# A two-layer attention and MLP kernel: the last queries of the first layer in two chunks, the last result block in three pieces, and a new order

## The chip, the cores and the metric

The kernel runs on one core of one Trainium2 chip. Its engines work side by side and meet only at semaphores: TensorE (PE in the profile; its weight loads are PEld), VectorE (DVE), ScalarE (ACT), GpSimd (POOL), and SyncE (SP), which issues the DMAs. The metric is device microseconds of one execution, as the median of several runs; lower is better.

## The reference

The input x has 2048 rows (positions) of 512 numbers. Two layers follow one another, with the same weights, and each has two halves:

```python
x = x + A(layernorm(x))     # attention: 32 heads of 16, causal, window of 256 positions
x = x + B(layernorm(x))     # an MLP over positions
x = x + A(layernorm(x))
x = x + B(layernorm(x))

# A: q, k, v = x @ wqkv;  p = softmax(mask(q k^T / 4));  out = (p v) @ wo
# B: h = layernorm(x);  u = gelu(h^T @ w1 + b1);  y = u @ w2 + b2;  out = y^T
#    w1 is 2048 x 1792, w2 is 1792 x 2048
```

The MLP mixes positions: its first product sums over all 2048 rows, so it can't be finished before the attention of the last row is done.

## The kernel before

Rows are kept as 16 blocks of 128 (x_sb, in bf16). A layer's attention is worked in chunks of queries, counted in units of 64: `CHUNKS` lists (start, length) pairs. The first layer has chunks of 256, 256, 512, 512 and 512 queries, the second layer four of 512.

For each chunk, `attention` (from about L645) takes the tiles of `attention_plan`. A tile holds eight pieces of 64 keys by 64 queries for four heads, side by side, and each goes through five steps: scores on TensorE (L689, 32-row matmuls, four heads at a time), the exponential on ScalarE (L704, two of 128x1024 a tile), masks on GpSimd or VectorE (L725), the product with V on TensorE (L746, 64-row matmuls of 17 columns of weights), and a finish of transpose, reciprocal, product and transpose on VectorE and GpSimd (L766, L770, L772, L777). A chunk of 512 goes through one head group at a time, with five tiles each; a chunk of 256 goes through pairs of head groups, and the two groups of a pair share their third tile, so a pair has five tiles. `wo_block` then multiplies by wo (through the helper at L512), adds to x_sb (L788), and normalises two blocks for the MLP (statistics L470 and L472, reciprocal root L483 on GpSimd, L490 on VectorE).

The first MLP product is split over blocks of rows so that part of it can run under the attention. In the first layer `u_part` sums blocks 0 to 3 and later blocks 4 to 11 as filler matmuls (L512, xh_sb by w1b), and `u_last` adds blocks 12 to 15 (L867), where two column tiles at a time hold two PSUM banks until all four blocks are in. The Gelu follows on ScalarE (L882). The second MLP product (`y_block`, L512 again, and L908) runs in the second layer under the attention's projections and at the end of the kernel alone. The last block of the result goes through `y_last` (L894, output DMA L897).

At the start, `f_warm` (L393) issues 42 matmuls on a constant tile. Meanwhile x and the weights are loaded, the first blocks are normalised and transposed on TensorE (L548), and the first projections follow. GpSimd builds constants and clears two key buffers (L460).

All operations are recorded first, in a graph with their reads, writes and buffers. Then `ORDER`, a compressed list of the operation to take next and of the engine that is to do it, is replayed: it fixes each engine's queue and which buffer each tile gets. The waits follow from the graph. The order was found offline; the kernel holds only its result.

Of the kernel before, what the change touches and what calls it, by code (L numbers as in the profile page):

```python
# [42 lines left out]

def begin_order(n):
# [260 lines left out]
def bass_interleave_layers__sliding_block__mixer_token_mlp__prompt_kernel(  # L305
# [11 lines left out]
    S, D = A_x.shape[1], A_x.shape[2]  # L317
    F = B_w1.shape[1]
# [3 lines left out]
    NFT = F // P  # L322
# [5 lines left out]
    SPLIT = [True, False]  # L328
    STAGED = [(1, 0), (2, 0), (3, 0)]

    CHUNKS = [[(0, 4), (4, 4), (8, 8), (16, 8), (24, 8)], [(0, 8), (8, 8), (16, 8), (24, 8)]]
    PARTS = [[(2, 0, 4), (4, 4, 12)], [(2, 0, 8)]]

    es = ExitStack()
    with es:
        sb = lambda name, shape, d=dt.bfloat16: es.enter_context(nc.sbuf_tensor(name, shape, d))
        x_sb = sb("x_sb", [P, NT, D])
# [14 lines left out]
        uT = sb("uT", [P, NFT, 512])  # L352
# [11 lines left out]
        b2col = sb("b2col", [P, NT], dt.float32)  # L364
# [5 lines left out]
        g = Graph(nc, es)  # L370
        op = g.op
# [17 lines left out]
        warm = Tile(banks)  # L389

        def f_warm(e):
            for _ in range(42):
                last = e.matmul(PS[:, warm.slot, 0:P], lhsT=uT[:, 0, 0:P], rhs=uT[:, 0, 0:P], start=True, stop=True)  # L393
            return last
        op("vector:wm", lambda e: e.memset(uT[:, 0, 0:P], 1.0), writes=["uT0"], cost=100)
# [13 lines left out]
        def load_w(i, a, b):  # L409
# [12 lines left out]
           cost=2600, prio=-1e6)  # L422
# [10 lines left out]
        for h in range(2):  # L433
# [5 lines left out]
               reads=["ident"], writes=[("half", h)])  # L439
# [19 lines left out]
        for k in (1, 2):  # L459
            op("gpsimd:zero", lambda e, k=k: e.memset(kbd[:, k].rearrange("p a b c d -> p (a b c d)").bitcast(dt.float32), 0.0),  # L460
               writes=["kz0"], cost=1900)
# [44 lines left out]
        def fprio():  # L506
            return 1e6 + len(g.ops)
# [10 lines left out]
        def mm_group(kind, dst, n, mk, reads, cols=512, step=2, prio=None, holds=(), after=()):  # L518

            prio = fprio() if prio is None else prio  # L520
            for k0 in range(0, n, step):
                k1 = min(n, k0 + step)

                def f(e, cols32, k0=k0, k1=k1):
                    last = None
                    for k in range(k0, k1):
                        last = matmul(e, cols32, *mk(k), start=(k == 0), stop=(k == n - 1))
                    return last
                rd = reads(k0, k1) if callable(reads) else reads
                op("tensor:" + kind, f, reads=rd, writes=[dst], cost=mm_cost(k1 - k0, cols), prio=prio, holds=holds, after=after, cfg="f",  # L530
                   cls="f", flex=True)
# [354 lines left out]
        def y_last(t):  # L886

            keys, w = w2t[t // 2]
            k = t % 2
            for c in (0, 256):  # L890
                ft = filler(True)
                mm_group("fy", ft, NFT, lambda fc, c=c, ft=ft: (bank(ft)[:, 0:256], w(fc)[:, k * P:(k + 1) * P], uT[:, fc, c:c + 256]),
                         lambda a, b: keys[a // 2:(b + 1) // 2] + [f"uT{fc}" for fc in range(a, b)], cols=256)
                op("vector:resy", lambda e, c=c, ft=ft: e.scalar_tensor_tensor(  # L894
                    x_sb[:, t, c:c + 256], bank(ft)[:, 0:256], b2col[:, t:t + 1], x_sb[:, t, c:c + 256], op0=ALU.add, op1=ALU.add),
                   reads=[ft, "b2", f"x{t}"], writes=[("y", t, c)], cost=dve_cost(256, psum=True, ptrs=1), prio=-2e5)
                op("sync:out", lambda e, c=c: e.dma_start(out_v[:, t, c:c + 256], x_sb[:, t, c:c + 256]), reads=[("y", t, c)],  # L897
                   dma=True, cost=600, prio=1e5)

        def y_block(t, wide):  # L900
# [11 lines left out]
        out_v = out.rearrange("b (t p) d -> p (b t) d", p=P)  # L912
        for layer in range(2):
# [24 lines left out]
            c0, _, b0 = PARTS[layer][-1]  # L938
# [49 lines left out]
```

## Time and profile before

| | |
|---|---|
| median of three runs | 440.72 us (439.57 to 442.05) |
| the profiled execution's own time | 439.72 us |
| its span, first to last instruction | 438.0 us |
| mean granted TensorE clock | 0.996 |
| busy: PE, DVE, ACT, POOL | 422.0, 324.0, 315.4, 187.8 us |
| exponentials (L704) | 304, 280.6 us |
| first exponential, last of the first layer | 12.36 us, 156.3 us |

The profile is that of one execution. Busy times of different engines overlap. A row of the timeline gives the start in us, the length in us, the engine, line and operation, the output and inputs, the shapes and the count; in brackets stands how long the engine had been idle and what released it. A row of the stages gives the stretch and its length, then the busy us (and instructions) of PE, PEld, DVE, ACT and POOL, the granted clock, the share of the DMA engines and GB/s.

### The profile page before, as it was taken

The page shows a single profiled execution, that of the slowest core. Times are in us where ns is not written, and L with a number is a line of the kernel's source. Part 1 is how long each engine was busy: PE and PEld are TensorE (multiplying, and loading weights), DVE is VectorE, ACT ScalarE, POOL GpSimd, SP SyncE. Part 2 cuts the span into 40 slices and gives each one's busy share as a digit, 9 for nine tenths or more (in the row PEclk, how much of TensorE's full clock was granted, in tenths as well). Part 3 has the DMA queues.
Part 4 walks back from the last instruction along what each step waited for, and adds up shares of the span by engine and source line. Part 5 has one row for each costly group of instructions (what it writes and reads, how often), then busy time and mean ns, then how long its engine had stood idle before and what let it go on. Part 6 is the DMA issues. An engine that isn't in the chain of part 4 may idle for free.

```text
span 438.0 us, 13924 instructions
## 1 busy us (share of the span) xinstructions
PE 422.0 (96%) x5976; PEld 187.2 (43%) x5976; DVE 324.0 (74%) x634; ACT 315.4 (72%) x360; POOL 187.8 (43%) x278
## 2 busy tenths in 40 slices
PE   6989988999989999999999999999999999999997
PEld 5543433333434444444344444444444444444443
DVE  6999888988988679565677999989888757520214
ACT  2999999999999932704989999999999980520000
POOL 6779976548582421010255554468556411000000
PEclk8999999999999999999999999999999999999999
DMA  8745552212252635643583152122324134668513
GB/s 235 151 88 76 136 100 65 67 22 55 46 131 54 165 84 169 180 123 85 143 127 86 36 131 69 22 62 41 73 50 121 53 100 131 192 187 244 159 36 120
DMA packets 106668, 46.13 MB, mean 105 GB/s; under 512 B 36848, under 2 KB 106608, under 8 KB 106608
## 3 DMA queue, kind: packets, MB, share of 16 engines
q1 hardware_dynamic: 106608, 45.26, 42.0%
q8 instruction: 47, 0.77, 0.8%
q14 instruction: 13, 0.11, 0.1%
HBM read 33.56 MB, written 2.10 MB: 81 GB/s over the span
## 4 chain that ended last, share of the span: by engine, by line
PE 81%; ACT 13%; DVE 4%; issue 1%; POOL 1%; DMA 0%
PE PS L512 56%; ACT pt L704 13%; PE PS L689 9%; PE PS L867 8%; PE PS L746 7%; DVE xh_sb L490 1%; DVE stats L470 1%; DVE x_sb L788 1%; DMA x_sb<-in_A_x_dram 0%; POOL pt L725 0%; DVE kbd L582 0%; DVE rl L766 0%; DVE agg L472 0%; DVE stg L593 0%; DVE qT L571 0%
## 5 line engine op out<-in xcount | busy, mean ns | idle before, releaser
L704 ACT ACTIVATE pt<-PS 128x1024 bf16<-128x1024 f32 (+1 forms) x304 | 280.6, 1039 | 9.8 <-PE PS L689 8.9
L725 POOL TENSOR_TENSOR pt<-pt,ldm 128x256 int32<-128x256 int32 (+2 forms) x195 | 130.5, 689 | 106.1 <-ACT pt L704 105.6
L512 PE MATMUL PS<-xhT,wqkv 128*128 128x512 bf16 (+1 forms) x288 | 68.2, 363 | 2.0 <-ACT pt L704 0.9
L512 PE MATMUL PS<-xh_sb,w1b 128*128 128x512 bf16 x280 | 69.6, 381 | 0.3 <-issue 0.2
L512 PE MATMUL PS<-uT,w2b 128*128 128x512 bf16 (+1 forms) x294 | 68.5, 370 | 0.0
L689 PE MATMUL PS<-qT,kbd 32*128 32x256 bf16 (+4 forms) x1488 | 60.4, 252 | 5.0 <-ACT pt L704 1.4
L908 DVE SCALAR_TENSOR_TENSOR x_sb<-PS,b2col,x_sb 128x512 bf16<-128x512 f32 x31 | 22.8, 745 | 43.7 <-PE PS L512 43.6
L483 POOL TENSOR_TENSOR rstd<-agg,mhalf 128x2 f32<-128x2 f32 (+1 forms) x33 | 22.9, 695 | 63.4 <-DVE agg L472 63.3
L689 PEld LDWEIGHTS PS<-qT,kbd 32*128 32x128 bf16 x1488 | 21.9, 93 | 63.4 <-ACT pt L704 44.6
L766 DVE STREAM_TRANSPOSE rl<-PS 128x1024 f32<-128x1024 f32 x32 | 39.8, 1243 | 10.5 <-PE PS L746 10.5
L882 ACT ACTIVATE uT<-rl,b1col 128x512 bf16<-128x512 f32 x28 | 18.2, 712 | 38.5 <-DVE rl L878 38.3
L746 PE MATMUL PS<-pt,vb 64*17 64x320 bf16 (+4 forms) x2976 | 43.3, 252 | 1.6 <-POOL pt L725 0.6
L470 DVE BATCH_NORM_STATS2 stats<-x_sb 128x6 f32<-128x512 bf16 x64 | 42.9, 682 | 1.4 <-DMA x_sb<-in_A_x_dram 0.6
L512 PEld LDWEIGHTS PS<-uT,w2b 128*128 128x128 bf16 x294 | 27.1, 98 | 31.6 <-issue 3.7
L512 PE MATMUL PS<-uT,pt 128*128 128x512 bf16 x168 | 40.4, 380 | 0.0
L725 DVE TENSOR_TENSOR pt<-pt,ldn 128x256 int32<-128x256 int32 (+1 forms) x75 | 28.7, 404 | 15.7 <-ACT pt L704 15.5
L746 PEld LDWEIGHTS PS<-pt,vb 64*17 64x17 bf16 x2976 | 30.8, 85 | 17.7 <-ACT pt L704 6.1
L867 PE MATMUL PS<-xh_sb,w1b 128*128 128x512 bf16 x168 | 37.7, 379 | 0.0
L512 PEld LDWEIGHTS PS<-xhT,wqkv 128*128 128x128 bf16 x288 | 24.6, 99 | 29.7 <-issue 5.6
L512 PEld LDWEIGHTS PS<-xh_sb,w1b 128*128 128x128 bf16 x280 | 23.4, 97 | 31.9 <-issue 7.2
L512 PE MATMUL PS<-wqkv,xhT 128*128 128x512 bf16 x128 | 34.1, 381 | 0.0
L512 PE MATMUL PS<-wo_sb,oT 128*128 128x512 bf16 x128 | 32.3, 380 | 0.7 <-ACT pt L704 0.5
(61 smaller groups left out, 338.1 us busy)
## 6 DMA issues: line engine op xcount, KB each, us to landing
w1b<-in_B_w_dram SPq DMA_DIRECT2D x112, 128.0 KB, 2.9
w2b<-in_B_w_dram SPq DMA_DIRECT2D x70, 128.0 KB, 2.9
pt<-in_B_w_dram SPq DMA_DIRECT2D x42, 128.0 KB, 2.8
vb<-vst SPq DMA_DIRECT2D x64, 68.0 KB, 2.1
out_dram<-x_sb SPq DMA_DIRECT2D x15, 128.0 KB, 1.8
x_sb<-in_A_x_dram SPq DMA_DIRECT2D x3, 512.0 KB, 7.5
kbd<-stg SPq DMA_DIRECT2D x88, 16.0 KB, 1.9
wqkv<-in_A_wqkv_dram SPq DMA_DIRECT2D x4, 256.0 KB, 4.2
```

Source lines behind the costliest of these rows:

```text
L470: op("vector:stat", lambda e: e.bn_stats(st[:, 0:6], x_sb[:, t, :]), reads=[f"x{t}"], writes=[("st", i)], cost=dve_cost(512))
L483: op("gpsimd:rstd", lambda e: e.tensor_tensor(rstd[:, t0:t1, 0], agg[:, t0:t1, 1], mhalf[:, 0:1].to_broadcast([P, t1 - t0]), op=ALU.pow), ...
L490: op("vector:xh", lambda e: e.tensor_scalar(xh_sb[:, t, :], x_sb[:, t, :], agg[:, t, 0:1], rstd[:, t, :], op0=ALU.subtract, op1=ALU.mult), ...
L512: return e.matmul(o, lhsT=w, rhs=x, start=start, stop=stop, skip_group_check=True)
L689: last = e.matmul(bank(tt[r // 2], r % 2)[:, base + c0 * 64:base + (c0 + n) * 64], lhsT=kbd[32 * r:32 * r + 32, tk.slot, o, jj].rearrange( ...
L704: op("scalar:exp", lambda e, ts=ts, tp=tp, i=i, cols=cols: e.activation(probs(tp)[:, i, 0:cols, :], pair(ts)[:, :, 0:cols].rearrange("p r ...
L725: return e.tensor_tensor(v, v, m, op=by)
L746: last = e.matmul(bank(t, h)[32 * r:32 * r + 17, i + q0 * 64:i + (q0 + n) * 64], lhsT=vb[64 * h:64 * h + 64, tk.slot, jj, 4 * o + r, :], r ...
L766: op("vector:od", lambda e, t=tod, tr=tr: e.transpose(rl[:, tr.slot:tr.slot + 2].rearrange("p a b -> p (a b)"), pair(t)), reads=[(tod, i) ...
L867: last = e.matmul(bank(tu, tt), lhsT=v()[:, sc - b0, k0 + tt * P:k0 + (tt + 1) * P], rhs=xh_sb[:, sc, :], start=(sc == b0), stop=(sc == NT ...
L882: op("scalar:gelu", lambda e, ft=ft, tt=tt: e.activation(uT[:, ft, :], rl[:, tmps[tt].slot], ACTF.Gelu_apprx_tanh, bias=b1col[:, ft:ft + 1 ...
L908: op("vector:resy", lambda e: e.scalar_tensor_tensor(x_sb[:, t, :], bank(ft), b2col[:, t:t + 1], x_sb[:, t, :], op0=ALU.add, op1=ALU.add), ...
```

## The change

Four things are edited. The last 512 queries of the first layer become two chunks of 256. The warm-up has 36 matmuls in place of 42. `y_last` computes the last block's 512 columns in pieces of 256, 128 and 128 in place of two of 256, each with its own accumulation, addition and output DMA. And `ORDER` is another string: every engine's queue, the choice of engine where an operation has one, and the buffers are fixed anew. Since the chunk list is counted by position, `u_part` over blocks 4 to 11 is now recorded after the first of the two new chunks.

```diff
 ORDER = (
-    'c-pO2F^KC{7QM2c=j(6YfM!uZS>AxMXh91KD2oCLD4;@F9MA^^T)0r-!i5VL+TcP9VsW7bFL*%#7cNvd;KGFiUhskg4!D?wSul$i9GJqz6cd=jg^MYsm|ga2'
...
+    'c-p;JO^D;j6@Id-yEWMw&_Fe4gBCQP1qC!g0R?nWf&yCbfCseT1P6T3fD*jmg98d^f(f3WfCF0aK?^$g;D9$c;D7@@IN*a1eej_ZI^cs3KJ>wdKJ=jjedt36'
...
 )

-    CHUNKS = [[(0, 4), (4, 4), (8, 8), (16, 8), (24, 8)], [(0, 8), (8, 8), (16, 8), (24, 8)]]
+    CHUNKS = [[(0, 4), (4, 4), (8, 8), (16, 8), (24, 4), (28, 4)], [(0, 8), (8, 8), (16, 8), (24, 8)]]
     PARTS = [[(2, 0, 4), (4, 4, 12)], [(2, 0, 8)]]

         def f_warm(e):
-            for _ in range(42):
+            for _ in range(36):

             keys, w = w2t[t // 2]
             k = t % 2
-            for c in (0, 256):
-                ft = filler(True)
-                mm_group("fy", ft, NFT, lambda fc, c=c, ft=ft: (bank(ft)[:, 0:256], w(fc)[:, k * P:(k + 1) * P], uT[:, fc, c:c + 256]),
-                         lambda a, b: keys[a // 2:(b + 1) // 2] + [f"uT{fc}" for fc in range(a, b)], cols=256)
-                op("vector:resy", lambda e, c=c, ft=ft: e.scalar_tensor_tensor(
-                    x_sb[:, t, c:c + 256], bank(ft)[:, 0:256], b2col[:, t:t + 1], x_sb[:, t, c:c + 256], op0=ALU.add, op1=ALU.add),
-                   reads=[ft, "b2", f"x{t}"], writes=[("y", t, c)], cost=dve_cost(256, psum=True, ptrs=1), prio=-2e5)
-                op("sync:out", lambda e, c=c: e.dma_start(out_v[:, t, c:c + 256], x_sb[:, t, c:c + 256]), reads=[("y", t, c)],
+            for c, d in ((0, 256), (256, 384), (384, 512)):
+                ft, n = filler(True), d - c
+                mm_group("fy", ft, NFT, lambda fc, c=c, d=d, n=n, ft=ft: (bank(ft)[:, 0:n], w(fc)[:, k * P:(k + 1) * P], uT[:, fc, c:d]),
+                         lambda a, b: keys[a // 2:(b + 1) // 2] + [f"uT{fc}" for fc in range(a, b)], cols=n)
+                op("vector:resy", lambda e, c=c, d=d, n=n, ft=ft: e.scalar_tensor_tensor(
+                    x_sb[:, t, c:d], bank(ft)[:, 0:n], b2col[:, t:t + 1], x_sb[:, t, c:d], op0=ALU.add, op1=ALU.add),
+                   reads=[ft, "b2", f"x{t}"], writes=[("y", t, c)], cost=dve_cost(n, psum=True, ptrs=1), prio=-2e5)
+                op("sync:out", lambda e, c=c, d=d: e.dma_start(out_v[:, t, c:d], x_sb[:, t, c:d]), reads=[("y", t, c)],
                    dma=True, cost=600, prio=1e5)
```

More of the change, by code (lines that the diff above doesn't have):

```diff
@@ new lines @@
+    'Nsxv^Ns?|_Qq<@siBHJ#eAX6|pGT8+?0KVAqw`@Zi-s-f@R3+ogTQ-Itd)pxs`##ZC1|Q@yO#XeK+}0ykQ7Bx1;X>oCDYZ(WO6bf0s%p|p((w}j4}c3^0HVg'
+    '+O^t@CyV8BITe-Z)Uu}Y`D{ihy&kPZe&%_8!aSakzS8UU`e*~CqwqYx(qe7FFXtq3Un-<P>h<wBo{T|);iyUnib7<W>vmlLk^@94h{8q~hQDbxghu<bSn!2v'
+    'gW$1ftzI3E-4Q8p&?{9c72Ez4o)On|P2056G%XYhh+OLVJui09%&=T`UC;`KTP~N4g6kU2Cx(Ie8aAaS8fCf$Ff>izq0{YJ9qUg3iNZf7Ac_D2Fp<@vR+D7O'
+    '^KJw|lBX-%E-Y*y0#LBYGFdD%P1lnIZU}(L;1Ls>%?_C~;r8DE?b|lGauY?%^Yil+RGVY3zgS#dr|H!dkki%QPfxpDf4NxZ7Or7TL+9*tdU`fL!$bO>H<(Yn'
@@ new lines @@
+    ')6;)U#*#Fj&kdtb{4e{R$;3B|cDr3MBD^I{)B9bc5w)TgIu^I%Hf_;Rr(r`am5QubtJf3-&k#~7pNC<Y{q*|uv{dq|zF#Vp0Ih(yAtQ^O4#v^~T*c&hmGDH6'
+    'X2J|8qYpDWQcY4Rd$OQiD#c0MP7nbKQHvZj8o{qDt5yTcGA%?^ED%C$3{SbFX#%zvOGPG<q-o#7ht>6pQl3yYJ4q78*ratFwc7$?Aq&u}uqlc)<VXNDQmeJg'
+    'GzN}5IIyfzv51FNk-=bFmLN(Z!fl#8jss(AOfyW=Rk~UMEN~vd4~!8tVLU>&rnJ|kFc?(7gf?`M%uo_ps};Qbb<lXxXf%*_L8t~NX6Dl`z|nQ<Y2n$^0x*_X'
+    'ifsJQkmb6}B<8BBR1acavb(n!Z9sT<Ifbz8$WjKGj+bt)4}P^+sd%QNu)1K4hQdG*`@M=`5a3l+Q!U(36lXI{tEiQ-wOXkXI)qjLiDjgVq9}EnO~#x6;SD+g'
@@ new lines @@
+    'rgGbHkj9uBaVci<r704is!Emq`N@eYIIgWZnw*&u$7x(2#<CnOqJG%vl##<FUy@|`^LmzI=F75)(PzD57oE3d)v|OmBZ)4{mPIes>c>^|;M1X^2}0NH9H-)='
+    'f}@u!<uGJj=;)91YP;Hsp7I22$F5eZMagptS=^s!n#MF0sHWi26iNvq(l|E68_=}NieVb(KnTc0Jef{Vem))yhkwmdE%To>9zt-&MG?Hb#pkPkHJdL1Fh_sM'
+    'Fh-&@)u+>`$5HwaF%l_283|M@N*5O>RmX6FN+M4elTi<3ne=9}Q~Vo9sGu+!e-{&dI1ImU{;}`aCZz_YUnohM0GBCTf28%>@qv7M+kxwANK-%}wLf13!8`~s'
+    '7?cXVQFf!u^AsgjXrYK2R1fBU9j#pU{U8i*_$Qh2$R?CP<O`b0t2|!?9}L~J<R4&Y03-?BouYdm4Uv%;^Xu#D<U>7<bw<^jn@4rzI5e9ifq4wA<74;?Ab5^T'
@@ new lines @@
+    '_ix2fJj54;Zlj_9)^U8_@kD$^HHU*AKkPp|nVn!396XqwOivsK>@2-ejCE9Dr`zKp?X*5e#aBoLtl$5k6|X&S^|BE4;%20zon*CA6s=xwwq~=qJ_Rt0AT$8!'
+    'hl-)=uB?>{Sj1c)GNNx<sHrHF>UjJ&HB|*cwrz>wY*D0w3RqasTgh=mm8p#MH9UtVNrZ@S9pV@UbSlyZ!temk)a~|FwadW)hoZuSFBs~JK+EMNl<3c%J-{{{'
+    'p*G=(nUEy&#e8vjdC9e5LdMJG5FPz<zf0pzr`rjKLue;$4oP3DHKQbPoY-kq%b1X1U=~bLtr-@kA~AFw)x4kys;UV3V^tXuj}VH-#@!xK6iDKd>zixSyrPDM'
+    'ywLT_v&(;;ot*;;13R6aS>vKC8SF2tKfq5HzgiVtRZ2)K2Et3|bb=RHD6ESl@*jB5JrBu}30bvPb;`wOwxegY>6!hBt?Rl|a8P;SM1Mjkef(IYxCuLsShJsz'
@@ new lines @@
+    'F^vPl@gZrD3&I7p8d+-`2y4r*!hC=wn+wJMMehRJ=Zkc{Nb!fn5VHo5o=D`hQwic`J*uPR1yB#_fLiQj4S^O*SO#URr*@@7Av8*5TPq+ujk1X~&hZ^gZIdq;'
+    '4oa{g>pEDO++Ziq3q+#*2!Tr{flOM6d!t=x7)n?L<u){xigH;a7=Rm(zap1s=1o~Xaf@f?!ICh0s`dLo#{-27Qrbx-lVqHbp*Wb_LLnLsBi8Q|n1me&%sQlD'
+    '6a=eUljwTG4yx5jYL9Gv5LbL_)U*;PWvA4rUar;3rmj|W09%nA)B{OXiAWR%BEt3Fjl(*$Yp(y^nu6-M_izBar$fkQ6Fw_jaCnfdaIjt|>*lhRdAMt!9pyJm'
+    '=a1I=WIb<fb(GI<S3knheE!u|hxyG}^4Obyw?Bt>UwnDnI=p{o4()zKHW+a4!fJiv?w+_UZeP)kfctv!+3uV*a@#1ach13m$IJo0@oUe!t*5!yySMMJ*W32r'
@@ L42 @@
+    'iwO|!ExK&M+B*Tq<-a{6b6*9aw*lwA8U6R(<lgXc4f+P^Z@&0_`*Gj&?f;`u{6Ox%Buj4Hg`K&B&F$5k+=g+R86VuSF1sFluzUSGuer&=p73zo2V?^j;W)A{'
+    'Li;S-N0E??MrG{FZyT^v0eFp-`F&m4b>=she4fw0{{CGvzwdu;n^E`XOm3HQx!u?rilcS=faA6tSj**p1|9A@wM)IjJO6er?+fz!e}=o7`i4)N%g%#6zxVEW'
+    '$nW=&{2L3vJA8w83~s$8x!vU48wBFGd)4EAWa-AXDf^ZVaj#~<s{}rJFQt*&25EDE{W|c5aB!~%U+cT0_)c12Z|eIi<?lyF-t)1(&e`{v!R@KSHmY0DcI_M%'
+    '!Oc)^-I==^&%OE$!tIr4?(0_TZ)^Vn<WV86'
 )
```

26 lines of the change are left out of this document (1 added, 25 removed).

## The prediction

> **What bounds the kernel now.** I read the page first, then the busy time by stage, then the timelines of the start, of the first layer's attention and of the end.
>
> ```profile
> PE 422.0 (96%) x5976; PEld 187.2 (43%) x5976; DVE 324.0 (74%) x634; ACT 315.4 (72%) x360; POOL 187.8 (43%) x278
> ```
>
> TensorE is busy for 422.0 of 438.0 us, so at most 16 us can be won without taking matmul work away. The stages (us, then busy us of each engine) say where those 16 lie:
>
> ```profile
> 12.36:131.00 118.64, 110.18 (x2212) 47.93 (x2210) 107.63 (x218) 116.38 (x129) 86.72 (x128) 1.00 0.41 85
> 131.00:156.40 25.40, 25.14 (x388) 10.40 (x388) 17.69 (x35) 24.35 (x28) 9.35 (x14) 1.00 0.38 101
> 156.40:204.00 47.60, 47.60 (x311) 21.64 (x310) 33.82 (x63) 13.36 (x19) 3.73 (x5) 1.00 0.53 146
> 204.00:357.50 153.50, 153.14 (x2615) 64.22 (x2613) 125.72 (x247) 147.16 (x164) 79.92 (x116) 1.00 0.34 77
> ```
>
> From the first exponential (12.36) to 131 ScalarE is the bound: 116.38 of 118.64 us, while PE idles 8.46 us. From 131 on, when the second MLP part (blocks 4 to 11) may start, PE is the bound: it idles 0.26 us to 156.4, nothing to 204 and 0.36 us to 357.5. So the time is "when 131 comes" plus "matmul work left at 131". A us won on ScalarE or at the start before 131 moves the end by a us; a us of PE work added after 131 costs a us.
>
> The start, which every exponential waits for:
>
> ```profile
> 1.10 4.51 PE L393 MATMUL PS<-uT 128*128 128x128 bf16 x42 [1.10 <-DVE stats L464]
> 5.43 2.65 DVE L490 TENSOR_SCALAR xh_sb<-x_sb,agg,rstd 128x512 bf16<-128x512 bf16 x1 [0.46 <-POOL rstd L483]
> 5.83 2.10 POOL L460 MEMSET kbd<- 128x2048 f32 x1
> 8.14 0.40 PE L548 MATMUL PS<-ident,xh_sb 128*128 128x128 bf16 x4 [2.31 <-DVE xh_sb L490]
> 9.05 2.74 PE L512 MATMUL PS<-xhT,wqkv 128*128 128x256 bf16 x12 [0.52 <-DVE xhT L555]
> 12.36 3.97 ACT L704 ACTIVATE pt<-PS 128x1024 bf16<-128x1024 f32 x5 [0.16 <-PE PS L689]
> ```
>
> The second block's normalising takes 2.65 us where its kind takes 465 ns on average: it lies beside a memset of GpSimd and ends when that has ended. PE idles 2.3 us, and then its granted clock is halved:
>
> ```profile
> 10.00:11.00 1.00, 1.00 (x7) 0.69 (x6) 0.02 (x1) 0.84 (x2) 0.00 (x0) 0.50 1.20 261
> ```
>
> The same twelve 256-column matmuls take 2.74 us here and 1.48 us at 12.24.
>
> **The change part by part.**
>
> **Two chunks of 256.** One chunk of 512 queries has 5 score tiles for each of 4 head groups, 20 in all; a chunk of 256 has 5 for each of 2 pairs, so two have 20 again, and 40 exponentials of 128x1024 either way: ScalarE gets nothing and loses nothing. The scores of a tile occupy PE for 0.33 to 0.34 us, whether they are 8, 12 or 24 matmuls: nothing. Mask operations go from 36 to 32 over the same columns: GpSimd has 16 us to spare between 131 and 156.4, so I take nothing. Products with V go from 12 to 16 pieces for each head group, 8 matmuls each:
>
> ```profile
> 35.03 1.53 PE L746 MATMUL PS<-pt,vb 64*17 64x64 bf16 x128 [0.56 <-POOL pt L725]
> ...
> 72.62 1.40 PE L746 MATMUL PS<-pt,vb 64*17 64x64 bf16 x96 [0.44 <-DVE vst L630]
> ```
>
> The first row is two head groups of the chunk of 256 at block 4: the next instruction starts 1.47 us later, so 0.74 us a group. The second is one group of a chunk of 512, 1.34 us by the same reading. Eight groups by 0.74 are 5.9 us, four by 1.34 are 5.4: **+0.6 us**, after 131 and so on the path. Were each group issued alone, 0.86 us for 56 matmuls (63.89) makes about 0.95 for 64, and the cost 2.2 us: the range is 0.6 to 2.2, and I take 0.6 because both pairs of the existing small chunk were issued together. Transposes, reciprocals, wo blocks and layer norms keep number and size; those of blocks 12 and 13 only come earlier.
>
> **Six warm-up matmuls fewer.** 6 by 107 ns (42 in 4.51 us) are 0.64 us of PE. The first transposes start at 5.44, behind the warm-ups, while their block was normalised at 4.97: they can start some 0.4 us earlier. But the projection at 9.05 also needs the second block, normalised only at 8.08: **nothing** on the path. If that block came without its delay, at about 5.9, the warm-ups would still not be last. What it could cost is a rival below.
>
> **Last block in three pieces.** 14 matmuls of 256 columns (0.109 us each, 12 in 1.48 less the pipeline's end of 0.17) become 28 of 128 columns. The nearest row is eight transposes of 128 columns at 17.43, 0.62 us with the same end: 0.056 each, so 28 make 1.57 against 1.53 us. The upper bound is the mean of a 128-column weight load, 98 ns: 2.74 us, +1.2. I take +0.04, since the transposes also load weights for every matmul. Behind the last matmul:
>
> ```profile
> 435.00 0.48 DVE L894 SCALAR_TENSOR_TENSOR x_sb<-PS,b2col,x_sb 128x256 bf16<-128x256 f32 x1
> 435.51 0.38 SPq L897 DMA_DIRECT2D out_dram<-x_sb  x1
> ```
>
> The addition falls from 0.48 to about 0.35 us (512 columns take 0.745, 256 take 0.484, so half of 256 saves 0.13). Outputs of 128 KB land in 1.8 us and of 64 KB in 1.6, so 32 KB might in 1.5; small packets speak against that: the 16 KB copies in rows of 128 B take 1.9. So -0.1 to +0.3. **Sum -0.2 us**, bounds -0.3 to +1.4. One more output DMA on SP costs 0.4 us of a queue with nothing behind it.
>
> The Trainium skill ("DMA: Bandwidth & Descriptors", Specifications) has 512 B as the smallest transfer for full rate, with read-modify-write below; the new rows are 256 B. It agrees with the sign of the 1.9 us row; by it the piece would come at the upper bound, +0.2 in place of -0.2.
>
> **The order.** It is a compressed string, so its content can't be read from the diff, yet it is the only part that reaches the large losses. What an order can remove before 131: 2.2 us of the starved normalising (2.65 less 0.465), by putting the memset elsewhere; with the gap gone, up to 1.3 us of half clock (2.74 less 1.48); ScalarE's 2.3 us of idle; and 0.9 us of its evictions (118.64 less 2.26 idle less 115.46 of exponentials). Together 6.7 us. What it can add: every one of these again, and the idle of the next part. From both sides -6.7 to +7; I take **-3.1**: the starved normalising, 2.2, and 0.9 of ScalarE's 3.2; the clock I leave as it is. I take this side because the losses stand at single places before 131, where the bracket names a neighbour that needn't be there, while the stages after 131 have no idle and lose only by a new wait.
>
> Sum on the profiled run's own 439.72 us (span 438.0): +0.6 -0.2 -3.1 = -2.7, 437.0. The median, 440.72, lies 1.0 above that run, so the forecast is 438.0.
>
> **The rivals.**
>
> *The order brings nothing.* Then +0.6 -0.2 remains: 441.1, the same. For it: PE is full from 131 to 435, and none of the edits reaches the wait at 5.43. Against it: an order found anew leaves no queue as it was.
>
> *The cover after the last exponential gets thin (slower).* Today, when the last exponential ends at 156.3, PE still holds MLP work that depends on nothing:
>
> ```profile
> 156.64 1.43 PE L746 MATMUL PS<-pt,vb 64*17 64x64 bf16 x96
> 158.00 3.63 PE L512 MATMUL PS<-xh_sb,w1b 128*128 128x512 bf16 x16
> 161.47 3.19 PE L512 MATMUL PS<-wo_sb,oT 128*128 128x512 bf16 x14
> ```
>
> 32 such matmuls (16 at 158.00, 8 at 164.49, 8 at 166.65) hide the chain up to the last normalised blocks. With the split the final MLP stage can begin early on blocks 12 and 13, and an order that trusts this may spend the 32 before. The chain for 256 queries is 0.74 (values), 1.25, 0.35, 0.69, 0.71 (DVE at 158.15 to 160.54), 8 wo matmuls by 0.216, then 0.67, 0.68, 0.18, 0.69 and two by 0.45: 8.6 us, of which PE works 2.5. Of the 6.1 left the final stage can cover 2.6: each pair of its tiles holds two of eight banks until blocks 14 and 15 come, with two banks kept for wo three pairs fit, 12 matmuls. So it wants 16 more; with none kept PE idles 3.5 us: 3.5 + 0.4 = 3.9, 444.6. It decides below some 8 kept (1.8 us idle). For it: the half clock after 2.3 us of idle at the start would come on top. Against it: today's order kept twice what is needed.
>
> *The clock.* Fewer warm-ups leave the gate shut for longer. Rows: half clock from about 8.7 to 12.1 costs 1.3 us on twelve matmuls. If the shorter burst brings one or two such stretches more, 1.3 to 2.6, I take 2.0: 2.0 + 0.4 = 2.4, 443.1, slower. Against it: with 36 the burst still lasts 3.9 us, the transposes follow, and the halving came behind an idle gap, not before the warm-ups' end.
> The Trainium skill ("TensorE: Matmul & The Clock Gate", The HAM clock gate) makes this a rule: the gate opens after a busy window of about 3.4 us and shuts after an idle one, free-running, so a shorter burst may miss a whole window. The trace agrees with a stretch of about 3.4 us, but here 2.3 us without work, and little after, were enough to shut it.
>
> **How the numbers follow.** The forecast has 0.42, the neutral order 0.24, the thin cover 0.28, the clock 0.06. About 0.5% (2.2 us: 438.5 and 442.9) can be told from no change by a measurement of this kernel. So faster 0.42, same 0.24, slower 0.34. The range goes from the whole 6.7 (440.7 - 6.7 + 0.4 = 434.4) to the thin cover with its upper bound, 445.0. The faster case alone spans 434.4 to 438.5.
>
> **What would show it.** Right: the normalising of the second block below 1 us, the first 128x1024 exponential near 10 us instead of 12.36, no row of half clock after 8 us; PE idle between the first exponential and the last at 7 us or less; products with V in rows of 128 matmuls near 1.5 us; the last addition near 0.35 us. Wrong: a PE gap of over 1 us between the last first-layer exponential and the final MLP stage (thin cover); half clock beyond 13 us (clock); or a start like today's with all else alike (neutral).

## The result and the profile after

The changed kernel takes 437.80 us (437.04 to 440.35), the kernel before in the same runs 440.43 us: a ratio of 0.9948 (95% interval 0.9933 to 0.9962), or 2.3 us less (1.7 to 3.0). The forecast was 438.0, and 437.80 lies below the 438.5 up to which the prediction counted its faster case (0.42). The profiled execution took 438.12 us; its span is 436.4 us and its granted clock 1.0.

The page's busy times of the changed kernel (busy us, share of the span, instructions):

```profile
span 436.4 us, 14227 instructions
PE 412.3 (94%) x6109; PEld 188.2 (43%) x6176; DVE 321.1 (74%) x628; ACT 316.4 (72%) x363; POOL 195.0 (45%) x284
```

PE seems 10 us less busy, but 67 matmuls are missing from this trace against the weight loads (6109 and 6176), and each leaves a gap in the record that need not be one on the chip. So this row, and PE's column in the stages, can't be set against those of before.

The stages of the changed kernel, cut as before (start:end, length, busy us and count of PE, PEld, DVE, ACT, POOL, then clock, DMA share, GB/s):

```profile
12.36:131.00 118.64, 107.00 (x2239) 47.51 (x2258) 104.17 (x205) 116.07 (x131) 88.66 (x129) 1.00 0.40 82
131.00:156.40 25.40, 24.73 (x480) 11.19 (x483) 19.73 (x39) 22.30 (x25) 10.78 (x13) 1.00 0.36 97
```

ScalarE still fills the first stretch: its idle is 118.64 less 116.07, 2.57 us, where it was 2.26 (the stretch now begins 2.36 us behind the first exponential). What changed lies ahead of it. The timeline of the changed kernel's start, rows of four engines:

```profile
2.19 4.02 PE L393 MATMUL PS<-uT 128*128 128x128 bf16 x36 [2.19 <-DVE uT L395]
5.43 0.41 DVE L490 TENSOR_SCALAR xh_sb<-x_sb,agg,rstd 128x512 bf16<-128x512 bf16 x1 [0.46 <-POOL rstd L483]
5.94 1.80 POOL L460 MEMSET kbd<- 128x2048 f32 x1
6.01 1.06 PE L548 MATMUL PS<-ident,xh_sb 128*128 128x128 bf16 x8
7.11 0.42 DVE L555 COPY xhT<-PS 128x512 bf16<-128x512 bf16 x1 [0.66 <-PE PS L548]
7.59 1.93 PE L512 MATMUL PS<-xhT,wqkv 128*128 128x256 bf16 x16 [0.52 <-DVE xhT L555]
10.00 3.02 ACT L704 ACTIVATE pt<-PS 128x1024 bf16<-128x1024 f32 x4
```

The second block is normalised in 0.41 us instead of 2.65. PE goes from the transposes to the projections with 0.52 us between, sixteen matmuls of 256 columns take 1.93 us, and the first exponential starts at 10.00 instead of 12.36. The stretch that ran at half clock before now reads 1.00 (same columns as the stages):

```profile
10.00:11.00 1.00, 1.00 (x12) 0.86 (x11) 0.97 (x4) 1.00 (x3) 0.88 (x2) 1.00 1.11 357
```

To see where a gain is kept, I take three marks from ScalarE's timeline: the starts of the first, the 33rd and the last (304th) exponential. The table holds all kernels but the two whose places don't fit their chunks.

| kernel (one profile each) | first | 33rd | last | span | 1st to 33rd | 33rd to last | last to end |
|---|---|---|---|---|---|---|---|
| before | 12.4 | 42.4 | 355.3 | 438.0 | 30.0 | 313.0 | 82.6 |
| m_wait | 12.4 | 43.0 | 355.6 | 438.4 | 30.6 | 312.5 | 82.8 |
| m_wait2 | 12.6 | 43.3 | 356.1 | 438.7 | 30.7 | 312.8 | 82.6 |
| w60 | 11.1 | 43.1 | 356.0 | 438.7 | 31.9 | 312.9 | 82.7 |
| after | 10.0 | 40.2 | 353.0 | 436.4 | 30.2 | 312.8 | 83.4 |
| after_again | 10.1 | 40.0 | 352.6 | 436.1 | 29.9 | 312.7 | 83.5 |
| a_w42 | 9.8 | 41.1 | 353.5 | 437.1 | 31.2 | 312.4 | 83.6 |
| a_y2 | 9.6 | 42.2 | 354.4 | 437.5 | 32.6 | 312.2 | 83.1 |
| h_layer | 10.0 | 42.6 | 355.3 | 438.0 | 32.6 | 312.8 | 82.7 |
| h_start | 9.2 | 39.7 | 353.8 | 436.4 | 30.5 | 314.1 | 82.6 |
| h_mid | 10.2 | 42.3 | 357.6 | 440.3 | 32.1 | 315.3 | 82.7 |
| h_back | 11.9 | 45.7 | 358.2 | 442.1 | 33.8 | 312.5 | 83.9 |

The profiled executions of a_w42, a_y2 and h_layer are the longest of six each, 0.9, 1.1 and 2.0 us above their medians.

Before and after differ by 2.2 to 2.4 us at the first and the 33rd exponential, by 0.2 from there to the last one, and the end takes back 0.7. The middle is a sum of two shifts. The last exponential of the first layer starts at 156.1 us, 0.9 later than before (155.2), and from there to the last one of all the changed kernel takes 196.9 us where before takes 200.1. PE has hardly a gap from 131 us on in either kernel, so what ScalarE loses there PE gains for other work.

### The profile page after: what moved, and what is told of

Read it like the earlier page. It is cut to its first block, busy times and chain, and to the rows that moved or that the text cites. A ratio compares the mean times of both kernels' runs of the same rounds, so it can differ in the third digit from the quotient of the medians.

```text
span 436.4 us, 14227 instructions
## 1 busy us (share of the span) xinstructions
PE 412.3 (94%) x6109; PEld 188.2 (43%) x6176; DVE 321.1 (74%) x628; ACT 316.4 (72%) x363; POOL 195.0 (45%) x284
## 4 chain that ended last, share of the span: by engine, by line
PE 74%; ACT 11%; DMA 5%; DVE 4%; SPq 3%; issue 2%; POOL 1%; POOLq 0%
PE PS L512 50%; ACT pt L704 11%; PE PS L689 8%; PE PS L867 7%; PE PS L746 7%; DMA wo_sb<-in_A_wo_dram 1%; DMA xhT<-xh_sb 1%; SPq L802 1%; DMA w1b<-in_B_w_dram 1%; PE PS L393 1%; DMA w2b<-in_B_w_dram 1%; SPq L541 1%; SPq L635 1%; DVE stats L470 1%; POOL kbd L608 0%
## 5 line engine op out<-in xcount | busy, mean ns | idle before, releaser
L704 ACT ACTIVATE pt<-PS 128x1024 bf16<-128x1024 f32 (+1 forms) x304 | 281.1, 1039 | 11.9 <-PE PS L689 11.1
L512 PE MATMUL PS<-uT,w2b 128*128 128x512 bf16 (+2 forms) x296 | 69.3, 359 | 1.4 <-issue 1.0
L512 PE MATMUL PS<-xhT,wqkv 128*128 128x512 bf16 (+1 forms) x274 | 64.8, 355 | 5.1 <-ACT pt L704 2.6
L512 PE MATMUL PS<-xh_sb,w1b 128*128 128x512 bf16 x266 | 66.9, 380 | 2.4 <-issue 1.8
L689 PE MATMUL PS<-qT,kbd 32*128 32x64 bf16 (+4 forms) x1552 | 60.2, 247 | 3.9 <-ACT pt L704 2.1
L908 DVE SCALAR_TENSOR_TENSOR x_sb<-PS,b2col,x_sb 128x512 bf16<-128x512 f32 x31 | 22.9, 743 | 43.3 <-PE PS L512 43.0
L746 PE MATMUL PS<-pt,vb 64*17 64x128 bf16 (+4 forms) x3104 | 43.9, 248 | 0.7 <-DVE vst L630 0.4
L512 PE MATMUL PS<-uT,pt 128*128 128x512 bf16 x164 | 42.1, 379 | 0.2
L746 PEld LDWEIGHTS PS<-pt,vb 64*17 64x17 bf16 x3104 | 31.7, 84 | 16.0 <-issue 5.7
L867 PE MATMUL PS<-xh_sb,w1b 128*128 128x512 bf16 x165 | 37.4, 379 | 0.2
L512 PE MATMUL PS<-wqkv,xhT 128*128 128x512 bf16 x117 | 31.9, 380 | 2.5 <-DMA xhT<-xh_sb 0.9
L725 DVE TENSOR_TENSOR pt<-pt,ldn 128x256 int32<-128x256 int32 (+2 forms) x71 | 27.7, 406 | 6.9 <-ACT pt L704 6.5
L512 PE MATMUL PS<-wo_sb,oT 128*128 128x512 bf16 x119 | 30.7, 380 | 2.2 <-issue 0.8
```

Of the source, the lines that this page charges most:

```text
L512: return e.matmul(o, lhsT=w, rhs=x, start=start, stop=stop, skip_group_check=True)
L689: last = e.matmul(bank(tt[r // 2], r % 2)[:, base + c0 * 64:base + (c0 + n) * 64], lhsT=kbd[32 * r:32 * r + 32, tk.slot, o, jj].rearrange( ...
L704: op("scalar:exp", lambda e, ts=ts, tp=tp, i=i, cols=cols: e.activation(probs(tp)[:, i, 0:cols, :], pair(ts)[:, :, 0:cols].rearrange("p r ...
L725: return e.tensor_tensor(v, v, m, op=by)
L746: last = e.matmul(bank(t, h)[32 * r:32 * r + 17, i + q0 * 64:i + (q0 + n) * 64], lhsT=vb[64 * h:64 * h + 64, tk.slot, jj, 4 * o + r, :], r ...
L867: last = e.matmul(bank(tu, tt), lhsT=v()[:, sc - b0, k0 + tt * P:k0 + (tt + 1) * P], rhs=xh_sb[:, sc, :], start=(sc == b0), stop=(sc == NT ...
```

## The experiments

The theory: the gain is the start's, made by the order of the first operations; the two chunks, the rest of the order and the warm-ups bring nothing. The rivals: it comes from the later order or the second layer; it comes from the clock alone; it is bound to the new chunks. Line numbers in the experiments' profiles differ by one or two, since `ORDER` has another length. In the edits, `A` is the changed kernel's list of operations, `B` that of before, and `rest(...)` the entries not yet taken, in their own order. Ratios are against the kernel before on the same chip, with 95% intervals.

**The order cut at three places.** These keep the old list's end and take the changed kernel's first operations, up to three cuts; all three have the last block in two pieces and 36 warm-ups.

```diff
 # h_start and h_mid keep the chunk (24, 8); h_layer has (24, 4), (28, 4)
-order = B
+order = A[:82] + rest(B)      # h_start: up to the 4th exponential
+order = A[:442] + rest(B)     # h_mid: up to the 63rd
+order = A[:1106] + rest(B)    # h_layer: the whole first-layer attention
```

> The kernel before (one chunk of 512, two pieces at the end), but the first operations in the changed kernel's order, up to its first four exponentials, and 36 warm-ups; all that follows in the order of before. Theory (the gain is the start: the second block's normalising no longer behind the memset, and no half clock): first exponential near 10.0 us, 2.4 us less than before, ratio about 0.9946. Rival one (the gain comes from the order between the start and the second MLP part): about half of it, 1.0 to 1.2 us. Rival two (the gain comes from the two chunks): no change.

Measured: 0.9960 (0.9944 to 0.9975), 1.8 us less of 440.19 (1.1 to 2.5), where 2.4 were expected. The first 82 operations, without the new chunks or the new pieces, bring about three quarters of the gain. The timeline of h_start's start:

```profile
5.35 0.41 DVE L489 TENSOR_SCALAR xh_sb<-x_sb,agg,rstd 128x512 bf16<-128x512 bf16 x1 [0.46 <-POOL rstd L482]
6.32 0.42 DVE L554 COPY xhT<-PS 128x512 bf16<-128x512 bf16 x1
6.82 1.91 PE L511 MATMUL PS<-xhT,wqkv 128*128 128x256 bf16 x16 [0.54 <-DVE xhT L554]
7.49 0.22 DVE L443 TENSOR_SCALAR ldm<-tri,half 128x64 int32<-128x64 bf16 x1
9.21 1.94 ACT L703 ACTIVATE pt<-PS 128x1024 bf16<-128x1024 f32 x2
```

VectorE copies the transposed block (L554, L555 in the changed kernel) ahead of the mask constant `ldm` (L443). This becomes important below. In this profile the 33rd exponential comes 2.7 us earlier than before, and 1.3 of them are lost in one wait of ScalarE for PE, 1.50 us at 45.01.

> As before, with the changed kernel's order for a longer beginning, up to its 63rd of 152 first-layer exponentials (some 65 us); still one chunk of 512 and two pieces. Theory: nothing beyond the start, 2.2 to 2.8 us less than before. Rival one (the order of the middle): more than the start alone, 3.0 to 3.7 us less. Rival two (the chunks): no change.

Measured: 1.0029 (1.0007 to 1.0051), slower. The cut itself costs: behind the seam, where the two orders meet, ScalarE waits once, in its timeline

```profile
82.24 3.77 ACT L703 ACTIVATE pt<-PS 128x1024 bf16<-128x1024 f32 x4 [2.15 <-PE PS L688]
```

and the 30 exponentials from the 63rd on take 30.4 us where before takes 28.0. So h_mid says what a joint between two orders costs, 2.4 us, and not what the operations up to the 63rd exponential are worth.

> The changed kernel's whole first layer (with the two chunks of 256) up to its last attention and part of the final MLP stage; the second layer and the end in the order of before, with two pieces. Theory: 2.4 less from the start, given back in part by the two chunks (0.5) and one more score tile after 128 us (0.4): 1.5 to 2.0 us less than before, less gain than with the start alone. Rival two (the chunks): the whole 2.6 us or more, and more than with the start alone.

Measured: 0.9941 (0.9918 to 0.9963), 437.74 us. With the second layer and the end in the old order the whole gain is there. The second layer's new order and the three pieces bring nothing that can be measured, and the rival that put the gain there falls. But 2.6 us (1.6 to 3.6) is more than the 1.5 to 2.0 that were expected, and it is what the rival of the two chunks was to give. Its interval overlaps with that of h_start, so the two runs don't say whether the chunks and the rest of the first layer's order add something.

**The other half alone.** The old start, and the changed kernel from there on:

```diff
+order = B[:82] + rest(A)      # h_back: 42 warm-ups, two chunks, three pieces
```

> The changed kernel (two chunks, three pieces, its order), but with the first operations in the order of before, up to six exponentials, and 42 warm-ups. Theory: first exponential at 12.3 us again, and the time back at that of before or up to 1 us above it (ratio 0.998 to 1.003). Rival two (the chunks) and rival one (the middle): 1 to 2.6 us less than before.

Measured: 1.0063 (1.0042 to 1.0084), 2.8 us slower. Again a seam: ScalarE has two gaps of 1.20 us, at 18.57 and 21.71, and the ninth exponential starts at 21.7 instead of 19.4. Less these 2.3 us it is the kernel before within its interval, which agrees with a back part that brings nothing, but a subtraction is no proof.

**The wait at 5.43 alone.** In the kernel before, the memsets of GpSimd are put behind one of the first two blocks' normalising.

```diff
+norms = [o for o in g.ops if o.kind == "xh"]
+for o in (one_memset, second_zero_memset): o.extra.append(norms[k])   # and behind it in ORDER
 # m_wait: k = 1;  m_wait2: k = 0
```

> The kernel before with two GpSimd memsets (the value buffer's ones and the second key buffer) made to wait for the second block's normalising, nothing else changed. Theory: the normalising takes 0.4 instead of 2.65 us, PE has no gap to lose its clock in, first exponential 2 to 3.5 us earlier, time 2 to 3.4 us less than before (ratio 0.992 to 0.995). Rival (the start is bound by weights that arrive, the normalising only seems to be last): the first exponential moves by less than 0.7 us and the time by as little.

Measured: 0.9993 (0.9974 to 1.0013). It missed its aim: block 1 is normalised first, so the memsets, free at 4.96, went ahead of the second block's reciprocal root on GpSimd. The timeline of m_wait:

```profile
4.96 0.64 POOL L456 MEMSET vst<- 128x128 bf16 x1 [0.35 <-DVE xh_sb L489]
5.21 2.10 POOL L459 MEMSET kbd<- 128x2048 f32 x1
7.28 0.57 POOL L482 TENSOR_TENSOR rstd<-agg,mhalf 128x1 f32<-128x1 f32 x1
7.88 0.41 DVE L489 TENSOR_SCALAR xh_sb<-x_sb,agg,rstd 128x512 bf16<-128x512 bf16 x1 [2.97 <-POOL rstd L482]
```

The normalising is short, but VectorE stands 2.97 us ahead of it, and it starts 2.45 us later than before (5.43). Short alone is not enough: it must be early too.

> The kernel before with two GpSimd memsets (the value buffer's ones and the second key buffer) made to wait for the block that is normalised second (the run m_wait had named the one normalised first). If the start alone carries the gain: the second normalising takes 0.4 us, first exponential at or before 10.5 us, time 1.5 to 2.4 us less than before, as with the changed kernel's first operations. Rival (what is won before the first exponential is given back between 17 and 43 us, as with 60 warm-ups): first exponential as early, but the 33rd as late as before, time within 0.7 us of before.

Measured: 1.0019 (0.9993 to 1.0045). This one hit its aim: the normalising takes 0.41 us at 5.45. Still nothing is won, and the first exponential, which both the theory and the rival had early, starts at 12.58. The timeline of m_wait2:

```profile
5.45 0.41 DVE L489 TENSOR_SCALAR xh_sb<-x_sb,agg,rstd 128x512 bf16<-128x512 bf16 x1 [0.46 <-POOL rstd L482]
6.16 2.11 POOL L459 MEMSET kbd<- 128x2048 f32 x1
8.23 0.29 POOL L441 TENSOR_SCALAR_AFFINE_SELECT tri<-tri 128x128 bf16<-128x128 bf16 x1
8.56 0.25 DVE L443 TENSOR_SCALAR ldm<-tri,half 128x64 int32<-128x64 bf16 x1 [2.70 <-POOL tri L441]
9.05 0.42 DVE L554 COPY xhT<-PS 128x512 bf16<-128x512 bf16 x1
9.53 2.46 PE L511 MATMUL PS<-xhT,wqkv 128*128 128x256 bf16 x12 [2.93 <-DVE xhT L554]
12.58 3.10 ACT L703 ACTIVATE pt<-PS 128x1024 bf16<-128x1024 f32 x4 [0.19 <-PE PS L688]
```

Read it from below. The projections wait 2.93 us for the copy of the transposed block; the copy stands in VectorE's queue behind `ldm`; `ldm` waits 2.70 us for `tri`; and `tri` stands in GpSimd's queue behind the memset. PE's stall is as long as before (2.31 and 0.52 us at two places there), and the twelve matmuls take 2.46 us instead of 1.48 again. The changed kernel has the copy ahead of `ldm` and `tri` ahead of the long memset, and clears `vst` on VectorE (0.17 us, on GpSimd 0.64).

**The clock alone.** More warm-ups in the kernel before, so that PE is busy up to the projections:

```diff
-            for _ in range(42):
+            for _ in range(60):     # w60
```

> The kernel before with 60 warm-up matmuls in place of 42, so that PE is busy until the second block is normalised at 8.1 us. Theory (the half clock is a cost of its own, 1.3 us on twelve matmuls): granted clock full from 8 to 12 us, the twelve 256-column matmuls near 1.5 us, first exponential 1 to 1.3 us earlier, time about 1 us less. Rival (the clock falls all the same, or the weights are last): no change, or later by what the warm-ups add.

Measured: 1.0001 (0.9985 to 1.0017). The clock did what was expected (timeline of w60):

```profile
9.06 1.48 PE L512 MATMUL PS<-xhT,wqkv 128*128 128x256 bf16 x12 [0.52 <-DVE xhT L555]
11.15 2.92 ACT L704 ACTIVATE pt<-PS 128x1024 bf16<-128x1024 f32 x4 [0.19 <-PE PS L689]
```

Twelve matmuls in 1.48 us, the first exponential 1.2 us earlier; but the 33rd starts at 43.1, no earlier than before (42.4). The chain of waits of w60 shows what came last in between (start, length, engine and line):

```profile
36.22 1.29 issue
38.15 0.69 DVE qT L571
39.44 1.57 DVE xh_sb L490 x2
41.66 1.04 PE PS L512 x4
```

A chain of VectorE's copies and normalisings stands there. ScalarE's timeline of w60 has the loss itself:

```profile
38.49 3.77 ACT L704 ACTIVATE pt<-PS 128x1024 bf16<-128x1024 f32 x4 [0.82 <-PE PS L689]
43.08 3.77 ACT L704 ACTIVATE pt<-PS 128x1024 bf16<-128x1024 f32 x4 [0.82 <-PE PS L689]
```

Up to the 28th exponential (36.65 us, before 37.88) the lead of 1.2 us is whole; these two waits use it up. What PE itself waited for at 36.22 ("issue", 1.29 us) the profile doesn't show.

**The changed kernel less one part.** a_w42 has the old number of warm-ups, a_y2 the old two pieces of the last block, after_again is the changed kernel in another set of runs.

```diff
-            for _ in range(36):                        # a_w42
+            for _ in range(42):
-            for c, d in ((0, 256), (256, 384), (384, 512)):   # a_y2
+            for c, d in ((0, 256), (256, 512)):
```

> The changed kernel with 42 warm-ups in place of 36. In the changed kernel the warm-ups start 1.1 us later than before and end at 6.0 us, behind the second block's normalising at 5.84. If that makes them last: transposes, first exponential and end 0.3 to 0.65 us later than the changed kernel. If the number of warm-ups matters to nothing (as I predicted): no difference. If a shorter burst harms the clock: earlier.

> The changed kernel with the last block in two pieces of 256 in place of 256, 128 and 128, the third piece's instructions left out of the order and the rest kept. In the changed order these pieces stand at 404 us, in the middle of the last matmuls, so no smaller last addition or transfer can count; 28 matmuls of 128 columns for 14 of 256 cost between 0.04 and 1.2 us of PE. Expected: the same time to 0.3 us less than the changed kernel.

> The changed kernel itself, for a second profile and for a ratio on the same chip as the three others. Expected ratio 0.993 to 0.996. In the first 17 us the same times as in its first profile to 0.3 us; between 17 and 43 us, where three engines and the DMA queue are all full, the 33rd exponential may differ by up to 2 us from its first profile (40.3 us), as it did between kernels that have the same order there (40.3, 41.1, 42.4).

Measured: a_w42 0.9925 (0.9902 to 0.9949), 437.95 us; a_y2 0.9933 (0.9909 to 0.9958), 438.21 us; after_again 0.9927 (0.9899 to 0.9955), 437.79 us. None can be told from the changed kernel. PE's timeline of a_w42:

```profile
2.19 4.28 PE L393 MATMUL PS<-uT 128*128 128x128 bf16 x42 [2.19 <-DVE uT L395]
6.31 0.61 PE L548 MATMUL PS<-ident,xh_sb 128*128 128x128 bf16 x8
```

The six more matmuls keep PE 0.3 us longer, and the eight transposes then take 0.61 us instead of 1.06: in both kernels they end near 7 us.

a_y2's profile shows something else. Its start is the changed kernel's, and yet its 33rd exponential comes 2.0 us later. Its chain of waits, then ScalarE's timeline:

```profile
26.15 4.08 DMA xhT<-xh_sb
```

```profile
32.77 3.77 ACT L702 ACTIVATE pt<-PS 128x1024 bf16<-128x1024 f32 x4 [2.19 <-PE PS L687]
```

A transposing DMA issued at 26.1 took 4.08 us to land, and ScalarE stood 2.19 us. a_y2's edit is at the other end of the kernel, so this is not its work. Between the two stands PE, in its timeline and in the stages of a_y2:

```profile
30.28 1.89 PE L510 MATMUL PS<-xhT,wqkv 128*128 128x512 bf16 x4 [1.99 <-DMA xhT<-xh_sb]
```

```profile
26.57:29.98 3.41, 1.35 (x84) 0.82 (x76) 3.27 (x8) 3.17 (x4) 3.41 (x4) 1.00 0.41 92
29.98:33.39 3.41, 3.11 (x14) 0.86 (x15) 0.94 (x2) 1.22 (x2) 2.83 (x5) 0.50 0.49 122
```

PE waited 1.99 us for the DMA, and then its granted clock was halved for 3.41 us: the eight projections of 512 columns took 1.89 and 1.39 us, where after_again's took 1.02 and 1.04. The same stretch of after_again:

```profile
28.29:31.70 3.41, 2.59 (x28) 0.81 (x20) 2.82 (x6) 3.41 (x5) 3.05 (x5) 1.00 0.41 105
```

The two other profiles of the new start that are late at the 33rd exponential show both things too: h_layer (the DMA 4.56 us, half clock from 31.05 to 34.46, ScalarE's wait 1.70 us) and h_mid (4.15 us, 31.94 to 35.35, 1.21 us). The half clock makes the eight projections 0.9 to 1.3 us longer, about half of the 1.8 to 2.2 us by which these three are late against the mean of after, after_again and a_w42 (40.4). In the four that are early (after, after_again, a_w42, h_start) this DMA, the last of a group of four, lands in 2.5 us and no stretch of half clock follows. In the four profiles of the old start it lands in 2.5 us as well, so they don't tell whether the old order would have borne a late one better. Why the DMA is late in some executions no run here shows.

The executions without a trace carry the same mark. Of the 40 of after, after_again, a_w42, a_y2 and h_layer, 33 have a mean granted clock of 0.999 or 1.0 and take 436.6 to 438.8 us; seven have 0.995 or 0.996, which is one such stretch in 437 us, and take 439.2 to 440.4. Where it lies in the five of the seven that have no trace is not shown.

**The chunks alone.** Each kernel with the other's chunks, the new operations standing at the places of those that they replace:

```diff
-    (24, 8)            # b_two256: the kernel before
+    (24, 4), (28, 4)
-    (24, 4), (28, 4)   # a_one512: the changed kernel
+    (24, 8)
```

> The kernel before with nothing changed but the last 512 queries of the first layer as two chunks of 256, their operations put at the places of the old chunk's. By my prediction's sum: 0.6 us more than before (bounds 0.6 to 2.2). Rival (the chunks bring the gain): 1 us or more less than before.

> The changed kernel with the last 512 queries as one chunk again, its operations put at the places of the two chunks', and what then isn't ready put off. By my sum: 0.5 us less than the changed kernel, if the places fit; with wo blocks of 12 and 13 now late, up to 2 us more. Rival (the chunks bring the gain): 1.5 us or more above the changed kernel, near the kernel before.

Measured: b_two256 1.0417 (1.0384 to 1.0450), a_one512 1.0328 (1.0298 to 1.0357): 18 and 14 us slower. The stages of b_two256 show where (columns as above; before's PE was busy 48.74 us of these 49):

```profile
131.00:180.00 49.00, 34.77 (x796) 15.19 (x797) 27.90 (x52) 30.26 (x32) 13.57 (x17) 0.98 0.28 75
```

PE stands 14 us: the places that one chunk shape was given don't suit the other. The two runs say that a chunk split needs an order of its own; they don't give the price of the split itself.

## Why the prediction was right, and where it wasn't

**The order, taken at -3.1.** -2.2 to -2.4 at the 33rd exponential. The place was right, but three things in this term were wrong, and in part they cancel.

The normalising ends 2.24 us earlier (5.84 for 8.08), as costed. The projections behind it start only 1.46 us earlier (7.59 for 9.05), because the transposes now wait for the warm-ups (until 6.01) and take 1.06 us. The other 0.9 us at the first exponential are the half clock, which the sum left as it was: from the first projection to the first exponential it is now 2.41 us instead of 3.31, with four more projections in it. w60 shows that a lead from the clock alone need not reach the end; no run has the new order at the old clock.

"By putting the memset elsewhere" is too small an edit: m_wait2 does just that and wins nothing, since `tri`, `ldm` and the copy wait next. The 2.2 us were the price of a queue order on two engines, not of one neighbour. And the 0.9 us taken from ScalarE's idle and evictions did not come: its idle before 131 went from 2.26 to 2.57 us.

How sure is the place? Over single profiles the stretch from the first to the 33rd exponential takes 29.9 to 32.6 us in the six kernels that have the changed kernel's order in all of it (after, after_again, a_w42, a_y2, h_layer, h_mid). Their mean start of the 33rd is 41.4 us, that of the four with the old order (before, m_wait, m_wait2, w60) 43.0: 1.6 us, and 1.9 to 3.0 for the three where the DMA is not late. From there to the last exponential the five without a seam take 312.6 us in the mean and the four 312.8. That h_start keeps 0.5 us less than the whole gain is inside the intervals; whether the rest of the first layer's order adds anything stays open.

**Two chunks, taken at +0.6.** The group price was right. PE's timeline of the changed kernel has the pairs issued together, 0.73 us a group:

```profile
137.86 1.53 PE L746 MATMUL PS<-pt,vb 64*17 64x64 bf16 x128
...
157.25 1.53 PE L746 MATMUL PS<-pt,vb 64*17 64x64 bf16 x128
```

The total shows no +0.6: 33rd to last is 313.0 before and 312.8 after. Something else in the order gave it back, or the spread hides it; no run settles which.

**Six warm-ups fewer, taken at nothing.** Right by a_w42. The reason given, that the warm-ups would "still not be last", is not: in the changed kernel they begin 1.1 us later than before, at 2.19, and end at 6.2, behind the second normalising (5.84). In a_w42 the transposes start later and run faster, as above, and end at the same time. That the longer burst made them faster isn't shown: after 36 they take 1.06 us in four profiles and 0.61 or 0.65 in two (h_start, a_y2), and those two have the earliest first exponentials, 9.2 and 9.6 us.

**The last block, taken at -0.2.** Wrong in sign, by the step "behind the last matmul". In the new order the three pieces don't stand last. The groups of line L894 of the changed kernel, then the end of its timeline:

```profile
L894 DVE SCALAR_TENSOR_TENSOR x_sb<-PS,b2col,x_sb x3: 343/351/484, 403.5 to 404.3; 128x128 bf16<-128x128 f32 x2, 128x256 bf16<-128x256 f32 x1
```

```profile
433.20 0.75 DVE L908 SCALAR_TENSOR_TENSOR x_sb<-PS,b2col,x_sb 128x512 bf16<-128x512 f32 x1 [0.54 <-PE PS L512]
432.69 1.63 SPq L954 DMA_DIRECT2D out_dram<-x_sb  x3
```

The 128-column additions take 0.343 and 0.351 us as estimated, but at 403.5 to 404.3 us, and the last one has 512 columns and takes 0.75 where before ended on 0.48. Last exponential to end: 83.4 to 83.6 us in the three profiles of the changed order with three pieces, 83.1 in a_y2, 82.6 before and 82.7 in h_layer. So the end costs 0.7 to 0.9, of which a_y2 gives back 0.2 to 0.5; with single profiles that is a sign, not a size. The outputs by issue (KB each, median us to landing):

```profile
out_dram<-x_sb SPq DMA_DIRECT2D x2, 32.0 KB, 1.9
out_dram<-x_sb SPq DMA_DIRECT2D x1, 64.0 KB, 1.7
```

Half the bytes take 0.2 us longer: 1.9 us, not the prediction's 1.5. The Trainium skill ("DMA: Bandwidth & Descriptors", Specifications) had this sign, with its slower writes below 512 B, and the trace agrees for rows of 256 B.

**The rivals.** Neutral: refuted by the ratio. Thin cover: the opposite of its sign shows in PE's timeline of the changed kernel behind the last first-layer exponential (157.16):

```profile
158.94 3.40 PE L512 MATMUL PS<-xh_sb,w1b 128*128 128x512 bf16 x15 [0.16 <-issue]
162.17 1.46 PE L512 MATMUL PS<-wo_sb,oT 128*128 128x512 bf16 x6
163.47 0.59 PE L867 MATMUL PS<-xh_sb,w1b 128*128 128x512 bf16 x2
```

By the weight loads, 24 of the second part's matmuls are still kept for after that exponential (23 show as matmuls; before: 32), the final stage (L867) starts between them, and no gap of PE there is over 0.2 us. Clock: no row of half clock from 8 to 13 us in the changed kernel. Its other sign, half clock beyond 13 us, does appear, in the executions with the late DMA above. There it follows a wait of PE; that the shorter burst has a part in it isn't shown. The sign "PE idle at 7 us or less" can't be read, because of the missing matmul records.

**The sum.** -2.7 forecast; -1.6 from span to span in the first pair of profiles, -1.9 with after_again, -2.3 by the ratio. That the total came this near is partly luck: of its terms the order brought 0.7 to 0.9 less than forecast, the end cost 0.9 more, and the chunks' 0.6 didn't show.

## What to carry to other kernels

A stall whose release is known is worth less than its length until the next wait on each in-order queue has been followed: with the normalising freed, the copy behind `ldm` kept the whole 2.2 us. Cost a reordering by the queues of all engines that meet there, and test it by joining two orders only with the price of the joint, here 2.3 and 2.4 us, in mind. And before costing a tail edit, ask whether the operation that it shortens will still be the last one.

## What the runs showed that was not expected

- **VectorE beside GpSimd.** The same normalising (128x512, bf16) takes 2.65 us in the kernel before, where GpSimd's memset starts 0.40 us into it and both end within 0.2 us of one another, and 0.41 us in the changed kernel, where the memset (1.80 us) starts 0.10 us after its end. In m_wait2 it is 0.41 us too, with the memset behind it. So engines can hold one another up without a semaphore between them. It doesn't hit every instruction: beside the changed kernel's memset (5.94 to 7.74) VectorE's statistics (0.69 us at 5.76) and its copy out of PSUM (0.42 us at 7.11) take no longer than elsewhere.
- **The spread of one stretch.** The first to the 33rd exponential takes 29.9 to 32.6 us under the same order, more than the whole gain; in the three late profiles the last transposing DMA of its group takes 4.08 to 4.56 us and a stretch of half clock follows, in the others it takes 2.5 us and there is none behind it.
- **An earlier first exponential need not count.** w60 brings it from 12.36 to 11.15 us by the clock alone and ends no earlier.
- **The clock.** 2.93 us without PE work in m_wait2, less than the window of about 3.4 us by which the Trainium skill ("TensorE: Matmul & The Clock Gate", The HAM clock gate) has the gate shut, and twelve matmuls took 2.46 us where they take 1.48 at full clock. The traces show more: the clock's records lie on a grid of 3.41 us. Over all kept traces that have such records, each of the 14 halved stretches inside a kernel follows a stretch of this grid in which PE was busy, by its records, for 14% to 45% of the time. One other stretch of 44%, at the end of a_y2, has no halving behind it, and neither has any of 50% or more. So in these runs it took a thin stretch, not an idle one.
